# Ordering three weight conversions behind the first batch's layer norm

## The chip, the cores and the metric

The kernel runs on one core of a Trainium2 chip. The metric is the time of one execution on the device, in microseconds. The kernel before takes 1025.44 us, the median of three runs (1022.24 to 1027.12). The work is shared out to TensorE (PE, matrix multiplication, results to PSUM), VectorE (DVE), ScalarE (ACT), GpSimd (POOL) and SyncE (SP, whose queue issues all the DMAs here). Each engine runs its own list of instructions strictly in order; engines wait for each other on semaphores.

## The reference

Three blocks follow each other, over a batch of four, 768 tokens and 384 channels:

```
a_n  = a * min(|a|, 0.999) / (|a| + 1e-6)             # complex, per token, head and channel
S_t  = a_n[t] * S_(t-1) + outer(k_t, v_t)             # 48 x 48 per head, t = 0 .. 767
y_t  = q_t @ real(S_t)                                # block 1: gated linear attention
u    = y + real(fft(fft(y, tokens), channels))        # block 2: Fourier mixer
un   = (u - mean(u)) / sqrt(var(u) + 1e-6)            #          layer norm over 384 channels
x    = u + relu(un @ w_ch1) @ w_ch2                   #          MLP, 384 -> 1536 -> 384
u2   = x + (relu(x^T @ w_tok1) @ w_tok2)^T            # block 3: token mixing, 768 -> 256 -> 768
out  = u2 + relu(u2 @ w_ch1') @ w_ch2'                #          MLP, 384 -> 1536 -> 384
```

## The kernel before, in words

For each batch there is a *chain* (block 1 and the mixer up to the layer norm: a scan of 48 steps on DVE with preparations on ACT and POOL, then chunks of small matmuls on PE, then the DFT by folding, and the norm) and the *dense* work (transposes of the normalised tokens, the first MLP, token mixing, the second MLP). In the dense work every fp32 product is split into high and low fp32r parts, three matmuls of 128 x 128 by 128 x 384 each. It is 936 such matmuls per batch: 432 in each MLP and 72 in the token mixing. An MLP goes in four quarters; a quarter takes three weight pairs, has 54 matmuls of the first layer (L1034, 18 per weight) and then 54 of the second (L1056). The chain of batch b+1 is meant to run beside the dense work of batch b. The chain of batch 0 has nothing beside it.

The weights come from DRAM as 64-bit floats and are split on the chip by `convert` (L199 to L244): a load (L206, SP), two or three ACT passes into PSUM and SBUF (L214, L219, L222), a step on DVE (L225 or L227), an addition on POOL (L229), a second DVE step for some (L233), a rounding on ACT (L239), a subtraction on POOL (L240) and a store of the two halves into the scratch `wscr` (L244). It is a Python generator with a `yield` between the stages, and `tick` moves every open one a stage on. The two steps that read PSUM tile `p` take turns in two PSUM buffers, so that the third conversion's ACT step L214 waits for the first one's L233. Tiles `cvt` take turns in eight SBUF buffers of tag T, which the transposed tokens `th` and `tl` use as well.

Eight conversions of weights (`early`) are over before the mixer of batch 0. Two of the next twelve (`back`) follow. Eight more are open when the mixer begins: their loads and the ACT steps L219 are issued by then, and five calls of `tick` at the end of `mirrors` (after L1137) issue the rest. Two (8,1 and 10,1) are issued after the layer norm by `feed(56)`. The 36 other weights are converted while batch 0's dense work runs, each just ahead of its use; the first of them, w1 of pair 4, is used after 126 of the dense matmuls. Weights of `back` are read again from the scratch (L320).

Names of the layer norm: L1152 is the last DFT matmul, L1188 copies its result from PSUM on ACT, L1189 and L1190 (POOL) form difference and sum, L1204 (DVE) adds the transposed input, in three rounds of two token tiles; L1211 and L1212 are statistics, L1221 to L1226 the inverse square root, L1233 (DVE) or L1231 (ACT) the normalised tile `un`. Then L1012 transposes it on PE, L1017 (ACT) and L1018 (DVE) split it into `th` and `tl`, and the first MLP begins at L1034. L347 are filler matmuls on PE ("warm").

What sets the order: the framework's list scheduler goes over a simulated timeline and takes, among what is ready, the instruction of lowest rank (`RANK`: conversions and dense work stand behind the chain). `after(x, y)` adds a dependency for this ordering alone, without a semaphore. `rest(x)` is `after(x, rests[0])` for DVE steps of a conversion; `rests[1]` does the same for the POOL addition. What the scheduler decides in one place shifts everything that it places later.

Of the kernel before, what the change touches and what calls it, by code (L numbers as in the profile page):

```python
# [54 lines left out]
def attn_fft_mixer_kernel(ctx: ExitStack, tc: tile.TileContext, aL, xL, vL, wL, qN, kN, vN, arN, aiN,  # L55
# [109 lines left out]
    LAST = [None]  # L165

    def marked(x):
        if stream[0] != CHAIN:
            mark[0] = x

    def after(x, y):
        tc.add_manual_dep(x.ins, y.ins.name, HOLD, reason="order of the streams")
# [6 lines left out]
    rests = [None, None]  # L179
# [72 lines left out]
    active, begun = [], []  # L252

    def begin():
        p, j = convs.pop(0)
        return convert(p, j, ws.place if (p, j) in early else None, far=True)

    def feed(n):

        keep, stream[0] = stream[0], BACK  # L260
        for _ in range(n):
            if convs:
                for _ in begin():
                    pass
        stream[0] = keep

    def tick(n, loads=False):

        keep, stream[0] = stream[0], BACK
        active[:] = [g for g in active if next(g, "end") != "end"]  # L270
        for _ in range(n):
            g = begin()
            next(g)
            if not loads:
                next(g)
            active.append(g)
        stream[0] = keep
# [790 lines left out]
    def stage2(b, space):  # L1068
# [50 lines left out]
        def dft(kt):  # L1119
            for ty in range(4):  # L1120
                n0, n = 128 * kt, ZK[ty][kt]
                ps = palloc("s", [128, 2, 97])
                for r in range(2):
                    for dt in range(2):
                        te.matmul(out=ps[0:n, r, :], lhsT=fd[:, ty, r, dt, n0:n0 + n], rhs=dcos[0:112, ty % 2, dt, r, :],
                                  start=(dt == 0), stop=(dt == 1))
                se.copy(out=Z[0:n, 2 * ty + kt, :].rearrange("p (i r) -> p r i", r=2), in_=ps[0:n])
# [7 lines left out]
        if b == 0:  # L1135
            for o, v in kept:
                after(sp.dma_start(out=o, in_=v), x)  # L1137
            marked(x)
            rests[0], rests[1] = x, None
            for _ in range(5):  # L1140
                tick(0)
            rests[0] = None
        dft(0)

# [165 lines left out]
    def on(s, f, *args):  # L1310
        stream[0] = s
        return f(*args)

    def chain(b):
        return stage2(b, stage1(b))
# [2 lines left out]
    sp.dma_start(out=fk, in_=cFk)  # L1318
    u, norm = on(FIRST, chain, 0)
    t1 = on(FIRST, transposed, u, norm, "s")  # L1320
    feed(56)
    for b in range(B - 2):
        lent[0] = int(not b)
# [21 lines left out]
    with tc.If(fv != 0):  # L1345
        with tc.For_i(0, B, 1) as b:
            fallback(b)
            u, norm = stage2(B, alloc("qk", [128, 12288], name="ws"))
            t = transposed(u, norm, "s")
            dense2(B, u, *dense1(B, u, *t), row=b)  # L1350
# [111 lines left out]
```

## Time and profile before

| what | us |
|---|---|
| median of three runs | 1025.44 |
| the profiled execution's own time | 1025.11 |
| its span, first to last instruction | 1023.2 |
| first matmul of the first MLP starts | 155.15 |
| busy: PE, DVE, ACT, POOL | 951.0, 716.9, 526.4, 452.8 |
| mean granted clock of TensorE | 0.991 of full speed |

Times in the trace are counted from the first instruction. Matmuls overlap, so the sum of their lengths (some 340 ns each) is about twice the time in which they pass; their count in a window gives the pace. The granted clock is 1.00 at 2.4 GHz and 0.50 at 1.2 GHz.

### The profile page before, as it was taken

To read this page: it belongs to the slowest core of one execution; us is meant where nothing else is said; L and a number is where in the kernel's file an instruction comes from. 1 tells how busy PE (TensorE), PEld (TensorE's weight loads), DVE (VectorE), ACT (ScalarE), POOL (GpSimd) and SP (SyncE) were. 2 spreads that over 40 slices of the span, in tenths; PEclk is the share of its full clock that TensorE was granted. 3 is DMA by queue.
4 is the path that set the end of the run, shared out by engine and by line. 5 is a ranking of instruction groups with operands and counts; after the bars stand their busy time and mean duration, and the time that the engine had idled before them with its cause. 6 is when DMAs were issued, how large, how long until landed. Compare 5 with 4: busy or idle time off the path is not lost.

```text
span 1023.2 us, 21015 instructions
## 1 busy us (share of the span) xinstructions
PE 951.0 (93%) x7312; PEld 902.0 (88%) x7312; DVE 716.9 (70%) x1965; ACT 526.4 (51%) x1489; POOL 452.8 (44%) x655
## 2 busy tenths in 40 slices
PE   1479989999899999999999999999999999999997
PEld 0338869999898899999998999999989999999997
DVE  7988978889897778999668889855664333433332
ACT  7864568887995166887216667821342122211111
POOL 7744677765785673677147335614630002000000
PEclk9999999999999999999999999999999999999999
DMA  6625865886689435665734467553325345435422
GB/s 234 175 67 140 290 269 165 283 268 210 212 258 272 146 95 187 193 179 174 206 110 140 129 193 247 157 149 102 108 78 166 131 131 171 139 108 176 136 91 80
DMA packets 98337, 173.09 MB, mean 169 GB/s; under 512 B 10928, under 2 KB 57904, under 8 KB 97712
## 3 DMA queue, kind: packets, MB, share of 16 engines
q1 hardware_dynamic: 98224, 171.67, 53.8%
q8 instruction: 60, 0.98, 0.4%
q14 instruction: 53, 0.43, 0.1%
HBM read 132.31 MB, written 39.32 MB: 168 GB/s over the span
## 4 chain that ended last, share of the span: by engine, by line
PE 66%; DVE 6%; ACT 3%; DMA 2%; POOL 2%; issue 2%; SPq 0%; POOLq 0%; ACTq 0%; DVEq 0%
PE l L1056 25%; PE l L1034 23%; DMA cvt<-wL 2%; PE s L845 2%; PE s L721 2%; PE l L1260 1%; PE l L1278 1%; PE s L1260 1%; PE s L1278 1%; PE s L1152 1%; DVE qkt L1099 1%; PE s L900 1%; PE s L860 1%; PE c L721 1%; PE c L845 1%
## 5 line engine op out<-in xcount | busy, mean ns | idle before, releaser
L1056 PE MATMUL l<-w,h 128*128 128x384 f32 x1728 | 324.0, 339 | 1.5 <-DVE h L1047 1.0
L1034 PE MATMUL l<-th,w 128*128 128x384 f32 x1152 | 313.3, 341 | 2.8 <-DVE h L1047 2.5
L1056 PEld LDWEIGHTS l<-w,h 128*128 128x128 f32 x1728 | 298.2, 188 | 3.5 <-DVE h L1047 2.0
L1034 PEld LDWEIGHTS l<-th,w 128*128 128x128 f32 x1152 | 209.1, 188 | 5.8 <-DVE h L1047 3.9
L1038 ACT ACTIVATE h<-l 128x384 fp32r<-128x384 f32 x192 | 94.0, 490 | 215.9 <-PE l L1034 215.3
L1034 PE MATMUL l<-tl,w 128*128 128x384 f32 x576 | 194.6, 338 | 0.0
L1059 DVE TENSOR_TENSOR u<-u,l 128x384 f32<-128x384 f32 x192 | 105.5, 549 | 74.4 <-PE l L1056 73.4
L1047 DVE SCALAR_TENSOR_TENSOR h<-l,h 128x384 fp32r<-128x384 f32 x160 | 88.3, 552 | 88.9 <-ACT h L1038 88.8
L1034 PEld LDWEIGHTS l<-tl,w 128*128 128x128 f32 x576 | 108.4, 188 | 0.1
L229 POOL TENSOR_TENSOR cvt<-cvt 128x384 int32<-128x384 int32 x48 | 50.4, 1051 | 27.4 <-DVE cvt L225 16.5
L1245 POOL TENSOR_TENSOR xl<-u,xh 128x384 fp32r<-128x384 f32 x18 | 18.0, 1014 | 93.2 <-ACT xh L1244 93.0
L240 POOL TENSOR_TENSOR w<-cvt,w 128x384 fp32r<-128x384 f32 x44 | 45.0, 1027 | 13.1 <-ACT w L239 13.0
L1045 POOL TENSOR_TENSOR h<-full,h 128x384 fp32r<-128x384 f32 x32 | 32.5, 1016 | 34.3 <-ACT full L1044 32.8
L529 PE MATMUL s<-misc,y 128*112 128x128 f32 x64 | 14.5, 369 | 35.4 <-DVE y L511 27.9
L694 DVE TENSOR_TENSOR p<-p,A 128x144 f32<-128x144 f32 x144 | 44.7, 310 | 2.8 <-ACT A L671 1.0
L529 PEld LDWEIGHTS s<-misc,y 128*112 128x112 f32 x64 | 9.3, 177 | 41.6 <-POOL ss L496 20.3
L881 POOL TENSOR_TENSOR yc<-Aa,gm 48x384 f32<-48x384 f32 x18 | 20.6, 1147 | 53.3 <-DVE Aa L871 53.0
L670 POOL TENSOR_TENSOR A<-raw,tm 128x144 f32<-128x144 f32 (+1 forms) x51 | 25.9, 508 | 39.4 <-DVE yt L695 29.6
L696 DVE TENSOR_TENSOR p<-p,yt 128x96 f32<-128x96 f32 x144 | 37.7, 262 | 2.8
L651 POOL TENSOR_TENSOR tm<-tm 128x144 f32<-128x144 f32 (+1 forms) x51 | 25.3, 496 | 32.3 <-ACT tm L650 27.8
L695 DVE TENSOR_TENSOR yt<-p,A 128x96 f32<-128x96 f32 x144 | 36.2, 251 | 2.4 <-ACT A L674 0.5
L721 PE MATMUL s<-misc,y 128*112 128x128 f32 x222 | 35.5, 273 | 1.2 <-DVE y L708 0.8
(320 smaller groups left out, 2045.2 us busy)
## 6 DMA issues: line engine op xcount, KB each, us to landing
w<-wscr SPq DMA_DIRECT2D x180, 384.0 KB, 3.5
cvt<-wL SPq DMA_DIRECT2D x48, 384.0 KB, 4.8
wscr<-w SPq DMA_DIRECT2D x44, 384.0 KB, 4.1
Kn<-kn SPq DMA_DIRECT2D x56, 192.0 KB, 3.7
kn<-y SPq DMA_DIRECT2D x96, 96.0 KB, 2.7
raw<-aL SPq DMA_DIRECT2D x48, 144.0 KB, 3.8
xx<-xL SPq DMA_DIRECT2D x48, 144.0 KB, 3.6
V<-vL SPq DMA_DIRECT2D x32, 144.0 KB, 3.0
```

The source lines that it names most:

```text
L229: x = ge.tensor_tensor(out=a, in0=a, in1=lo, op=ALU.add)
L240: ge.tensor_tensor(out=parts[:, 1, :], in0=a.bitcast(F32), in1=r32(parts[:, 0, :]), op=ALU.subtract)
L694: ve.tensor_tensor(out=cur, in0=prev, in1=A[:, j, 0:3, :], op=ALU.mult)
L695: ve.tensor_tensor(out=y, in0=prev[:, 1::-1, :], in1=A[:, j, 3:5, :], op=ALU.mult)
L696: ve.tensor_tensor(out=cur[:, 0:2, :], in0=cur[:, 0:2, :], in1=y, op=ALU.add)
L721: te.transpose(ps[:, j, :], y[:, j, 0:112], ident)
L1034: te.matmul(out=ps, lhsT=w1[:, wi, kt * 128:kt * 128 + 128], rhs=x[g][:, kt, :], start=(n == 0), stop=(n == 8))
L1038: x = se.activation(out=hi, in_=ps, func=ACTF.Relu)
L1045: ge.tensor_tensor(out=lo, in0=full, in1=r32(hi), op=ALU.subtract)
L1047: ve.scalar_tensor_tensor(out=lo, in0=ps, scalar=0.0, in1=r32(hi), op0=ALU.max, op1=ALU.subtract)
L1056: te.matmul(out=ps, lhsT=hs[m][:, hi, tt * 128:tt * 128 + 128], rhs=w2[:, wi, :], start=(n == 0), stop=(n == 8))
L1059: ve.tensor_tensor(out=u[tt], in0=u[tt], in1=ps, op=ALU.add)
```

## The change

Of the eight open conversions the first five run on as before. The last three, cvt_1380, cvt_1382 and cvt_1384 in the built program (weights 15,1, 4,1 and 6,1), are set aside during the five ticks and put back into `active`. They are ticked after the transposes of batch 0 have been issued, with their DVE steps and the POOL addition ordered behind `LAST[0]`, the last normalised tile of batch 0 (L1231, token tile 5). What follows from these steps by data (L239, L240, the store L244) is behind it as well. Their loads and first ACT steps are issued where they were.

```
--- before.py
+++ after.py
@@ -1137,8 +1137,10 @@
                 after(sp.dma_start(out=o, in_=v), x)
             marked(x)
             rests[0], rests[1] = x, None
+            active[:], begun[:] = active[:5], active[5:]
             for _ in range(5):
                 tick(0)
+            active[:], begun[:] = begun[:], []
             rests[0] = None
         dft(0)
 
@@ -1318,6 +1320,10 @@
     sp.dma_start(out=fk, in_=cFk)
     u, norm = on(FIRST, chain, 0)
     t1 = on(FIRST, transposed, u, norm, "s")
+    rests[:] = [LAST[0]] * 2
+    for _ in range(5):
+        tick(0)
+    rests[:] = [None] * 2
     feed(56)
     for b in range(B - 2):
         lent[0] = int(not b)
```

(From here on, lines of the changed kernel are two higher than before between L1139 and L1322, and six higher behind.)

How the built programs differ. On DVE, in the layer norm of batch 0, the rows around the normalisation of the first token tile (u0) stood so before; cvt is a conversion's tile, p its PSUM tile:

```order
L227 TENSOR_SCALAR cvt_1384<-p_1473 128x384
L1204 TENSOR_TENSOR u1_1509<-s_1734,qkt_278 128x192
L1204 TENSOR_TENSOR u4_1512<-c_1743,qkt_278 128x192 x2
L1211 BN_STATS bst_1683<-u1_1509 128x6
L1225 TENSOR_TENSOR l_1712<-l_1712,rs_1685 128x2
L233 SCALAR_TENSOR_TENSOR cvt_1382<-p_1470,cvt_1382 128x384
L1211 BN_STATS bst_1683<-u4_1512 128x6
L1212 BN_AGGR mv_1684<-bst_1683 128x2
L1226 SCALAR_TENSOR_TENSOR rs_1685<-l_1712,rs_1685 128x2
L1212 BN_AGGR mv_1684<-bst_1683 128x2
L1233 TENSOR_SCALAR qkt_278<-u0_1508,mv_1684,rs_1685 128x384
```

Now the three conversions stand on DVE behind the last normalised tile there, between the splits of the transposed tokens (tl, th):

```order
L1018 TENSOR_TENSOR tl_1792<-s_1799,th_1790 128x3x128
L227 TENSOR_SCALAR cvt_1380<-p_1467 128x384
L227 TENSOR_SCALAR cvt_1382<-p_1470 128x384
L1018 TENSOR_TENSOR tl_1791<-c_1807,th_1789 128x3x128
L233 SCALAR_TENSOR_TENSOR cvt_1380<-p_1467,cvt_1380 128x384
L1018 TENSOR_TENSOR tl_1792<-s_1813,th_1790 128x3x128
L1018 TENSOR_TENSOR tl_1791<-s_1819,th_1789 128x3x128
L227 TENSOR_SCALAR cvt_1384<-p_1473 128x384
L1018 TENSOR_TENSOR tl_1792<-c_1825,th_1790 128x3x128
L233 SCALAR_TENSOR_TENSOR cvt_1382<-p_1470,cvt_1382 128x384
```

All six DVE instructions have moved; no conversion is left between the first statistics and the last normalised tile.

On SP's queue, the stores of the conversions (wscr) and the loads of the next (cvt from wL) stood so before, up to the first loads for weights that the dense work waits for (cvt_3574 is w1 of pair 4):

```order
L244 DMA wscr150_134<-cvt_1378 128x768
L244 DMA wscr151_135<-cvt_1380 128x768
L244 DMA wscr41_113<-cvt_1382 128x768
L244 DMA wscr61_117<-cvt_1384 128x768
L206 DMA cvt_1851<-wL 128x768
L206 DMA cvt_1862<-wL 128x768
L626 DMA raw_1920<-aL 128x288
L630 DMA xx_1922<-xL 128x288
L244 DMA wscr81_121<-cvt_1851 128x768
L244 DMA wscr101_125<-cvt_1862 128x768
L206 DMA cvt_3574<-wL 128x768
```

and now:

```order
L244 DMA wscr150_134<-cvt_1378 128x768
L206 DMA cvt_1851<-wL 128x768
L626 DMA raw_1920<-aL 128x288
L630 DMA xx_1922<-xL 128x288
L244 DMA wscr151_135<-cvt_1380 128x768
L206 DMA cvt_1862<-wL 128x768
L244 DMA wscr41_113<-cvt_1382 128x768
L244 DMA wscr61_117<-cvt_1384 128x768
L206 DMA cvt_3574<-wL 128x768
L244 DMA wscr81_121<-cvt_1851 128x768
L206 DMA cvt_3582<-wL 128x768
```

The loads of cvt_1862 and cvt_3574 now stand behind the stores of moved conversions.

## Rows read from the trace of the kernel before

**Rows 1.** the page, part 1: busy time, share and instructions.

```profile
PE 951.0 (93%) x7312; PEld 902.0 (88%) x7312; DVE 716.9 (70%) x1965; ACT 526.4 (51%) x1489; POOL 452.8 (44%) x655
```

**Rows 2.** windows of 20 us: length, busy us (count) by engine, clock, DMA.

```profile
160.00:180.00 20.00, 20.00 (x119) 19.92 (x118) 17.71 (x49) 17.76 (x52) 15.86 (x24) 1.00 0.63 212
...
380.00:400.00 20.00, 20.00 (x125) 19.15 (x124) 15.80 (x54) 10.56 (x29) 1.50 (x4) 1.00 0.36 110
```

**Rows 3.** waits of PE, 155 to 390 us: total us, times, longest.

```profile
PE l L1034 <- DVE h L1047: 2.3, 2, 1.6
PE p L1125 <- DVE qkt L1109: 1.7, 2, 1.5
PE s L845 <- DVE gt L813: 1.6, 1, 1.6
```

**Rows 4.** timeline of PE, start of the first MLP: start, length, line, operation.

```profile
155.15 1.34 PE L1034 MATMUL l<-th,w 128*128 128x384 f32 x3
...
157.89 0.51 PE L1034 MATMUL l<-th,w 128*128 128x384 f32 x2
```

**Rows 5.** windows of 2 us around it.

```profile
150.00:152.00 2.00, 2.00 (x4) 0.42 (x2) 1.15 (x5) 1.97 (x9) 0.00 (x0) 0.50 0.95 313
...
156.00:158.00 2.00, 2.00 (x13) 1.98 (x12) 1.08 (x3) 2.00 (x7) 1.17 (x2) 1.00 0.16 45
```

**Rows 6.** instruction groups, 126 to 155 us: busy, mean ns, idle before.

```profile
L229 POOL TENSOR_TENSOR cvt<-cvt 128x384 int32<-128x384 int32 x8 | 8.1, 1019 | 7.3 <-DVE cvt L227 7.3
L240 POOL TENSOR_TENSOR cvt<-cvt 128x384 fp32r<-128x384 f32 x8 | 8.0, 1005 | 2.3 <-ACT cvt L239 2.3
...
L233 DVE SCALAR_TENSOR_TENSOR cvt<-p,cvt 128x384 int32<-128x384 int32 x8 | 4.4, 551 | 2.3 <-POOL cvt L229 2.1
L227 DVE TENSOR_SCALAR cvt<-p 128x384 int32<-128x384 int32 x8 | 4.3, 552 | 1.5 <-ACT p L214 1.5
L239 ACT CAST cvt<-cvt 128x384 fp32r<-128x384 f32 x8 | 4.0, 501 | 1.1 <-DVE cvt L233 1.1
```

**Rows 7.** timeline of ACT.

```profile
140.89 0.48 ACT L1188 COPY qkt<-s 128x386 f32<-128x386 f32 x1
...
151.76 0.72 ACT L1231 ACTIVATE qkt<-u,rs 128x384 f32<-128x384 f32 x1
...
390.80 0.71 ACT L1231 ACTIVATE qkt<-u,rs 128x384 f32<-128x384 f32 x1
```

**Rows 8.** timeline of POOL.

```profile
142.56 1.01 POOL L229 TENSOR_TENSOR cvt<-cvt 128x384 int32<-128x384 int32 x1
143.53 0.53 POOL L1189 TENSOR_TENSOR qkt<-qkt 128x193 f32<-128x193 f32 x1
...
172.84 1.08 POOL L240 TENSOR_TENSOR w<-cvt,w 128x384 fp32r<-128x384 f32 x1
```

**Rows 9.** timeline of DVE.

```profile
143.45 2.26 DVE L1233 TENSOR_SCALAR qkt<-u,mv,rs 128x384 f32<-128x384 f32 x1
...
146.17 0.61 DVE L1204 TENSOR_TENSOR u<-s,qkt 128x192 f32<-128x192 f32 x2
...
151.17 0.48 DVE L1233 TENSOR_SCALAR qkt<-u,mv,rs 128x384 f32<-128x384 f32 x1
...
167.79 0.32 DVE L694 TENSOR_TENSOR p<-p,A 128x144 f32<-128x144 f32 x1
```

**Rows 10.** the window from the first scan step of POOL to L240.

```profile
152.88:173.92 21.04, 21.04 (x115) 20.11 (x114) 16.46 (x40) 18.93 (x53) 14.88 (x22) 0.93 0.44 146
```

**Rows 11.** timeline of PE, end of batch 0.

```profile
394.98 2.70 PE L1056 MATMUL l<-w,h 128*128 128x384 f32 x14
```

**Rows 12.** timeline of the DMA queue of SP.

```profile
148.55 0.88 SPq L206 DMA_DIRECT2D cvt<-wL  x2
...
163.87 2.62 SPq L206 DMA_DIRECT2D cvt<-wL  x4
```

**Rows 13.** DMA issues, 100 to 230 us: count, size, us to landing.

```profile
wscr<-cvt SPq DMA_DIRECT2D x12, 384.0 KB, 3.7
```

More of the change, by code (lines that the diff above doesn't have):

```diff
@@ L1139, in stage2 @@
             rests[0], rests[1] = x, None
+            active[:], begun[:] = active[:5], active[5:]
             for _ in range(5):
                 tick(0)
+            active[:], begun[:] = begun[:], []
             rests[0] = None
@@ L1320, in attn_fft_mixer_kernel @@
     t1 = on(FIRST, transposed, u, norm, "s")
+    rests[:] = [LAST[0]] * 2
+    for _ in range(5):
+        tick(0)
+    rests[:] = [None] * 2
     feed(56)
```

## The prediction, made before the changed kernel ran

> **What bounds the kernel now.** Read the page's busy times first: PE is busy for 951.0 of 1023.2 us [rows 1]. Then the windows of 20 us: from 160 to 180 PE passes 119 matmuls, nearly all dense, so one in 0.168 us, and from 380 us on it stands full (125 matmuls, some of them small) to the end [rows 2]. The end is thus the start of the first MLP, plus PE's fixed work, plus what PE waits behind that start. The waits between 155 and 390 us are 12 rows with 12.3 us in sum, of which the three largest stand in [rows 3]; behind 390 there is little. Third, the start: the first dense matmul begins at 155.15 and the 13th at 157.89 [rows 4]. Twelve at 0.168 us are 2.0, so PE is where a full-rate start at 155.9 would put it. The rest is clock: 0.50 granted from 150 to 152 us (1.2 GHz), 1.00 from 156 to 158 (2.4 GHz) [rows 5]; PE had waited for tiles of the layer norm before.
>
> So there are two questions: how much earlier PE starts, and whether it must wait more afterwards.
>
> **What leaves the layer norm.** Three conversions take with them 3 L227 and 3 L233 on DVE (6 x 0.55 = 3.3 us), 3 L229 and 3 L240 on POOL (3 x 1.019 + 3 x 1.005 = 6.1 us), 3 L239 on ACT (1.5 us) and three stores on SP [rows 6]. One L214 goes later too, as its PSUM buffer is freed later. None of this work disappears.
>
> What of it lay on the path? Follow the third round of the norm. Its copy L1188 comes from PE and stays: 140.89 + 0.48 = 141.37 [rows 7]. POOL's L1189 starts only at 143.53, because L229 of a moved conversion holds POOL from 142.56 [rows 8]. Without it the two additions of 0.53 end at 142.45, against 144.5: 2.1 us. On DVE, L1233 of the first tile takes 2.26 us beside these POOL instructions and 0.48 later, when POOL is idle; then a moved L233 follows, and L1204 of the third round starts at 146.17 [rows 9]. Now L1233 would be held at most until 142.45, end at 142.95, and with one small step L1204 starts at 143.1: 3.1 us earlier. From 146.17 to the last normalised tile (151.76 + 0.72 = 152.48) it is 6.3 us [rows 7, 9]; less an L239 in ACT's way, that tile is done at 149.0, 3.5 us earlier.
>
> On ACT two scan steps of about 0.4 and three L1017 of 0.48 follow: the first MLP can start at 151.1. But the order puts four ACT steps of conversions and scan, at the 0.50 of L239 some 2.0 us, ahead of the last L1017, which the tenth matmul needs: it comes at 153.5, nine matmuls are through at 152.6, PE waits 0.9. The effective start is 152.0 against 155.9: **-3.9**. Bounds: -2.1, if only POOL's share is won and the clock falls as before; -4.8 without the wait of 0.9.
>
> What this L1233 shows bears on the moved work too. The Trainium skill, SBUF — State Buffer, section SBUF: two separate sides, says that VectorE and GpSimd take a shared pair of ports as an exclusive lock, in some forms of operation, and the later one is blocked for the whole instruction. The trace agrees in the 2.26 us. By that rule the moved additions take the lock from the scan's DVE steps instead; it is the mechanism of the second rival.
>
> **What comes back behind it.**
> (a) *PE's wait for L813.* PE waits 1.6 us at L845, where the chain of batch 1 leaves its scan [rows 3]. Counted over the built programs, 747 dense matmuls stand ahead of that place before and 771 now: 24 x 0.168 = 4.0 us more cover, about as much as PE starts earlier. If the scan is no later than before, the wait goes: **-1.6** (bounds -1.6 and 0).
> (b) *The first weights converted in the MLP.* POOL's L240 for w1 of pair 4 ends at 172.84 + 1.08 = 173.9 [rows 8]; PE needs it after 126 matmuls, at 155.9 + 21.2 = 177.1. There were 3.2 us to spare. Now PE needs it at 173.2. From the first scan step to this L240 POOL was busy for 14.9 of 21.0 us [rows 10], and the moved 6.1 us join it. Starting at 149.3 (3.6 earlier, with the norm), they end at 170.3 if they fill all of POOL's idle time and at 176.4 if none. PE waits 0 to 3.2 us there; I take the middle, and as the next weights follow at the same distance nothing is won back: **+1.5**.
> (c) *The scan and the end of batch 0.* DVE is busy for 17.7 of 20 us at 160 to 180 [rows 2], and the scan's first step (167.79 before [rows 9]) has moved steps ahead of it, 3.3 us on DVE. I put it 2.5 us earlier, less than PE. Besides, 14 dense matmuls stood behind the last transposes of batch 1 [rows 11], and now none does, 2.4 us less cover; but the tile that they transpose was ready at 390.80 + 0.71 = 391.5 [rows 7], 3.2 us before PE turned to it. Other waits grow by 0 to 2.4: **+1.0**.
>
> The sum is -3.9 - 1.6 + 1.5 + 1.0 = -3.0. The profiled execution took 1025.1 us (its span and 1.9 around it), 0.3 below the median of the runs. I forecast 1022.
>
> **The rivals.**
> *PE alone decides.* All of POOL's idle time is used, (b) and (c) are 0, and L1034's waits for DVE (2.3 us, [rows 3]) shrink by half: -3.9 - 1.6 - 1.1 = -6.6, so 1018.5. For it: PE is full from 380 on. Against it: the loads below.
> *Given back in the scan.* The moved work of DVE and POOL slows the stretch in which DVE is 88% busy: 3.3 us of its own and up to 1.8 (2.26 - 0.48, [rows 9]) for a block, one such. That is 5.1, against the 5.5 of -3.9 and (a): the time stays at 1025. For it: conversions, scan and dense steps share DVE, ACT and POOL, and every one of them runs in order. Against it: the order has 24 more dense matmuls before the scan's end, so PE has work while it lasts.
> *Slower: SP's queue.* The loads cvt_1851 and cvt_1862 were issued together at 148.55, four loads of the next weights from 163.87 [rows 12]. Now cvt_1862 takes the buffer of cvt_1380 and waits until its store has landed (3.7 us [rows 13]); behind it stand two more moved stores and the load for w1 of pair 4. If POOL's 6.1 and this 3.7 both go into the stream of conversions, that weight comes at 173.9 + 9.8 = 183.7, 6.6 us after the old need of 177.1, and PE's early start is worth nothing: 1025.1 + 6.6 = 1032. It decides from the point at which L240 for w1 of pair 4 ends later than 177.1. Against it: POOL and the queue start 3.6 us earlier, and the store's landing lies beside POOL's other work.
> That the change doesn't do what it says is excluded by the order of DVE and SP: the steps have moved.
>
> **How the numbers follow.** Forecast 0.45, PE alone 0.22, given back 0.20, slower 0.13. About 0.5% (5.1 us) is what a measurement of this kernel tells from no change. Faster by more than that needs less than 1020.3: 0.8 of the PE case and a quarter of the forecast's, 0.29. Slower by more than that needs over 1030.6: most of the last case, 0.12. The rest, 0.59, is within. With the terms' bounds the forecast alone goes from 1018.7 (-4.8 - 1.6) to 1026.6 (-2.1 + 3.2 + 0.4); with most of the PE case and a part above, the range is 1017 to 1028.5.
>
> **What would show it.** In the profile after: the last normalised tile ends near 149 and the first L1034 starts near 151 (within 1 us), without a stretch of clock 0.50 as long as before; POOL's first addition of the third round follows its copy on ACT at once; w1 of pair 4 is done between 171 and 176; PE has little or no wait at L845 of batch 1, and the last matmul of batch 0 ends 2 to 4 us before 397.7. I am wrong if L1034 starts after 153.5, if PE's waits between there and 390 are over 15 us in sum, or if the difference arises behind 400 us, where I see nothing that changes.

## The result

The changed kernel takes 1033.96 us, the median of 11 runs (1029.37 to 1040.03), against 1025.11 for the kernel before on the same chip (11 runs, 1022.24 to 1027.12): a ratio of 1.0094, interval 1.0075 to 1.0112. It is slower by some 9 us, where 3 us less were forecast, and above the top of the range. The profiled execution took 1031.89 us (span 1030.0, granted clock 0.988), so its span is 6.8 us longer than before; the other 2 us between the medians are not in this trace.

The page of the changed kernel, part 1, has the same 7312 matmuls:

```profile
PE 955.5 (93%) x7312; PEld 904.5 (88%) x7312; DVE 716.1 (70%) x1965; ACT 526.7 (51%) x1489; POOL 453.9 (44%) x655
```

Against [rows 1] TensorE is busy 4.5 us longer with the same work and idle 2.3 us longer (1030.0 - 955.5 = 74.5 against 1023.2 - 951.0 = 72.2).

**The head came out as forecast.** The timelines of PE, ACT and POOL of the changed kernel: start, length, line, tiles.

```profile
150.94 0.74 PE L1034 MATMUL l<-th,w 128*128 128x384 f32 x1
```

```profile
140.86 0.48 ACT L1190 COPY qkt<-s 128x386 f32<-128x386 f32 x1 [1.22 <-PE s L1154]
...
147.71 0.71 ACT L1233 ACTIVATE qkt<-u,rs 128x384 f32<-128x384 f32 x1
...
151.70 0.51 ACT L1017 CAST th<-c 128x384 fp32r<-128x384 f32 x1
```

```profile
141.42 0.53 POOL L1191 TENSOR_TENSOR qkt<-qkt 128x193 f32<-128x193 f32 x1 [1.74 <-ACT qkt L1190]
...
171.52 2.06 POOL L240 TENSOR_TENSOR w<-cvt,w 128x384 fp32r<-128x384 f32 x2
```

POOL's addition follows its copy at once (141.42 behind 141.34), the last normalised tile is done at 148.4 (152.5 before, [rows 7]), and the first dense matmul starts at 150.94 instead of 155.15 [rows 4]. The traces of the experiments below agree: with the head of before (before, e2, e3, e8) the first dense matmul starts at 153.8 to 156.5 us, with the changed head (the changed kernel, e1, e5, e7, e9, e12, e13) at 150.5 to 153.9. Windows of 2 us of the changed kernel, in the columns of [rows 5], show the clock at its upper level where it had been at 0.50:

```profile
150.00:152.00 2.00, 1.91 (x9) 1.29 (x10) 1.99 (x5) 2.00 (x6) 2.00 (x4) 1.00 0.28 77
```

The waits of PE from 155 to 390 us, in the columns of [rows 3]:

```profile
PE l L1034 <- DVE h L1047: 3.5, 4, 1.9
PE l L1056 <- DVE h L1047: 1.8, 2, 1.2
PE l L1012 <- DVE u L1282: 1.4, 1, 1.4
PE s L860 <- DMA Kn<-kn: 1.3, 1, 1.3
```

L845's wait for L813 is gone. The ten rows add to 10.8 us; the twelve of before add to 10.3, not to the 12.3 of the prediction. The first h (L1038) is 4.6 us earlier than before, the 49th, at 397 us, still 2.1 us.

**The loss lies behind 480 us.** First the waits of PE from 480 to 800 us before, the rows of the layer norm, then those of the changed kernel:

```profile
PE c L1012 <- ACT qkt L1231: 0.8, 1, 0.8
PE s L1012 <- ACT qkt L1231: 0.5, 1, 0.5
```

```profile
PE s L1012 <- ACT qkt L1233: 3.8, 1, 3.8
PE s L860 <- DMA Kn<-kn: 2.5, 1, 2.5
```

Two waits are new in size: 2.5 us at 498 us, where the chunks of batch 2 need their first Kn, and 3.8 us at 767 us, where TensorE has no dense matmul left and waits for the layer norm of batch 3. Behind each the clock falls. Windows of the changed kernel (length, busy us and count of PE, PEld, DVE, ACT, POOL, clock, DMA), and two of them before:

```profile
496.00:500.00 4.00, 1.65 (x34) 1.63 (x35) 1.33 (x3) 0.00 (x0) 0.00 (x0) 0.95 0.66 202
500.00:504.00 4.00, 4.00 (x21) 3.89 (x21) 3.37 (x8) 0.48 (x1) 0.00 (x0) 0.62 0.77 203
...
764.00:768.00 4.00, 0.70 (x4) 0.71 (x5) 3.41 (x5) 3.24 (x8) 3.72 (x4) 0.73 0.46 174
768.00:772.00 4.00, 4.00 (x14) 4.00 (x14) 0.71 (x2) 1.07 (x2) 2.06 (x3) 0.50 0.02 4
```

```profile
500.00:504.00 4.00, 4.00 (x59) 3.74 (x59) 2.42 (x5) 0.95 (x2) 1.63 (x2) 1.00 0.65 183
...
768.00:772.00 4.00, 4.00 (x25) 4.00 (x24) 1.11 (x2) 0.55 (x2) 0.00 (x0) 1.00 0.38 105
```

Last, the chain's own clock: ACT's last normalised tile of batches 1, 2 and 3 in the changed kernel (the first column is its start), and of batches 2 and 3 before; that of batch 1 before is the last of [rows 7], 390.80.

```profile
392.45 0.71 ACT L1233 ACTIVATE qkt<-u,rs 128x384 f32<-128x384 f32 x1 [0.23 <-DVE rs L1232]
...
589.07 0.70 ACT L1233 ACTIVATE qkt<-u,rs 128x384 f32<-128x384 f32 x1
...
768.19 0.71 ACT L1233 ACTIVATE qkt<-u,rs 128x384 f32<-128x384 f32 x1 [0.95 <-DVE rs L1232]
```

```profile
583.42 0.71 ACT L1231 ACTIVATE qkt<-u,rs 128x384 f32<-128x384 f32 x1 [0.23 <-DVE rs L1230]
...
762.22 0.70 ACT L1231 ACTIVATE qkt<-u,rs 128x384 f32<-128x384 f32 x1
```

From the last of these to the end of the span it is 261.0 us before and 261.8 after. So the 6.8 us are: 1.65 late at batch 1, 4.0 more from batch 1 to batch 2, 0.3 from there to batch 3, 0.8 behind. The 1.65 is within what executions differ by: e9 and e12 below have the changed kernel's order up to there, and in their traces that tile starts at 398.7 and 393.1. TensorE's dense work is 3.2 us early at 479 us (its 1369th matmul) and 2.1 us late at 590 (its 1657th).

Where batch 2 loses its 4.0 us is seen at its stations: the first and the last step of its scan (the 48 steps on DVE), the first matmul of the chunks (L803) and the first that needs Kn (L860). Before, then the changed kernel:

```profile
397.27 0.32 DVE L694 TENSOR_TENSOR p<-p,A 128x144 f32<-128x144 f32 x1
484.59 0.31 DVE L694 TENSOR_TENSOR p<-p,A 128x144 f32<-128x144 f32 x1
...
488.71 0.65 PE L803 MATMUL s<-misc,ends 128*48 128x64 f32 x16
494.95 0.26 PE L860 MATMUL s<-V,Kn 96*64 96x48 f32 x1
```

```profile
396.38 0.32 DVE L694 TENSOR_TENSOR p<-p,A 128x144 f32<-128x144 f32 x1
486.56 0.31 DVE L694 TENSOR_TENSOR p<-p,A 128x144 f32<-128x144 f32 x1
...
488.96 0.43 PE L803 MATMUL s<-misc,ends 128*48 128x64 f32 x8
498.35 0.23 PE L860 MATMUL s<-V,Kn 96*64 96x48 f32 x1 [2.53 <-DMA Kn<-kn]
```

The scan starts 0.9 us earlier than before and ends 2.0 us later; the chunks begin 0.25 us late, their first Kn product 3.4 us, and the norm comes 5.65 us late.

The two built programs also differ in what stands ahead of the chain in TensorE's queue. Number of dense matmuls there (the last columns: how many stand between the chain's last transposes L1199 of batch 3 and TensorE's stop for the last normalised tiles, behind the 2304th):

| dense matmuls ahead of | before | after | cover of the last norm, before | after |
|---|---|---|---|---|
| first L803 (chunks begin), batches 1, 2, 3 | 747, 1399, 2068 | 771, 1412, 2079 | | |
| first L1125 (mixer), batches 1, 2, 3 | 824, 1507, 2199 | 854, 1530, 2213 | | |
| last L1199, batch 3 | 2260 | 2272 | 44 | 32 |

24 to 30 more dense matmuls stand ahead of the chain of batch 1 and 13 to 23 more ahead of that of batch 2. That the chain is late because it stands behind them is not what the traces show. From the last y of the scan (L708) to the first L803 it is 6.1 us in both kernels at batch 1 (302.22 to 308.31 before, 306.33 to 312.41 now), and at batch 2 it is 4.5 us before (484.22 to 488.71) and 2.8 now (486.19 to 488.96): it is the scan that ends later. The last columns do bear on the last norm: 12 matmuls less of cover are 2.0 us at 0.168 [rows 2], and the wait there is 2.5 us longer (3.8 against 0.8 + 0.5).

### The profile page after: what moved, and what is told of

Read it like the earlier page. It is cut to its first block, busy times and chain, and to the rows that moved or that the text cites. A ratio compares the mean times of both kernels' runs of the same rounds, so it can differ in the third digit from the quotient of the medians.

```text
span 1030.0 us, 20993 instructions
## 1 busy us (share of the span) xinstructions
PE 955.5 (93%) x7312; PEld 904.5 (88%) x7312; DVE 716.1 (70%) x1965; ACT 526.7 (51%) x1489; POOL 453.9 (44%) x655
## 4 chain that ended last, share of the span: by engine, by line
PE 45%; DVE 3%; POOL 1%; DMA 1%; ACT 1%; issue 1%; POOLq 0%; SPq 0%
PE l L1034 17%; PE l L1056 17%; PE s L845 1%; PE s L1262 1%; PE s L1280 1%; POOL qkt L1109 1%; DMA kn<-y 1%; PE s L721 1%; PE s L900 1%; DVE qkt L1099 1%; PE s L1154 1%; PE c L845 1%; PE s L1012 1%; PE s L860 0%; PE s L906 0%
## 5 line engine op out<-in xcount | busy, mean ns | idle before, releaser
L1038 ACT ACTIVATE h<-l 128x384 fp32r<-128x384 f32 x192 | 94.4, 493 | 210.2 <-PE l L1034 209.6
L240 POOL TENSOR_TENSOR w<-cvt,w 128x384 fp32r<-128x384 f32 x44 | 45.6, 1044 | 15.9 <-ACT w L239 15.6
```

Source lines behind the costliest of these rows:

```text
L240: ge.tensor_tensor(out=parts[:, 1, :], in0=a.bitcast(F32), in1=r32(parts[:, 0, :]), op=ALU.subtract)
L1038: x = se.activation(out=hi, in_=ps, func=ACTF.Relu)
```

## The experiments

Theory A: the loss comes from the order behind the change. Rival B: it comes from the moved steps, which load the scan of batch 1. Most runs use a table of an engine's instructions by their numbers of issue in another built program; each is ordered behind its predecessor there, by dependencies without a semaphore, so that a stretch can be given the order of either kernel:

```
-            return getattr(self.eng, name)
+            return wrapped(getattr(self.eng, name), pin)   # pin(x) after each instruction
...
+            if a in made and b in made:                    # a, b: neighbours in the table
+                tc.add_manual_dep(made[b].ins, made[a].ins.name, HOLD, reason="order of before")
```

All times, with the stages of the chain in the profiled execution (start of the last normalised tile, as above). Each ratio is to runs of before on the same chip; the row of before is that of the first comparison.

| run | median us | ratio to before, interval | profiled us | batch 1 | 1 to 2 | 2 to 3 | 3 to end |
|---|---|---|---|---|---|---|---|
| before | 1025.1 | | 1025.1 | 390.8 | 192.6 | 178.8 | 261.0 |
| changed | 1034.0 | 1.0075 to 1.0112 | 1031.9 | 392.4 | 196.6 | 179.1 | 261.8 |
| e1_order_before | 1032.9 | 1.0060 to 1.0105 | 1031.1 | 396.5 | 192.9 | 178.8 | 261.0 |
| e2_order_after | 1034.5 | 1.0080 to 1.0120 | 1040.7 | 399.4 | 199.2 | 179.1 | 261.2 |
| e3_null | 1039.0 | 1.0111 to 1.0152 | 1039.8 | 392.6 | 195.7 | 179.1 | 270.5 |
| e4_move_two | 1030.3 | 1.0038 to 1.0071 | 1030.8 | 389.7 | 196.5 | 182.5 | 260.3 |
| e5_conv_free | 1029.7 | 1.0027 to 1.0059 | 1028.5 | 394.3 | 192.6 | 178.8 | 260.9 |
| e6_two_free | 1027.8 | 1.0014 to 1.0049 | 1026.8 | 392.8 | 192.6 | 178.8 | 260.8 |
| e7_kn_early | 1047.8 | 1.0201 to 1.0248 | 1047.5 | 403.8 | 198.7 | 179.2 | 264.0 |
| e8_null_act | 1036.1 | 1.0070 to 1.0126 | 1036.0 | 392.1 | 196.9 | 178.3 | 266.8 |
| e9_before_from_batch2 | 1025.7 | 0.9978 to 1.0015 | 1029.0 | 398.7 | 189.1 | 178.8 | 260.7 |
| e10_head_plus4 | 1032.7 | 1.0045 to 1.0100 | 1032.6 | 394.2 | 196.2 | 179.1 | 261.2 |
| e11_one_free | 1028.6 | 1.0004 to 1.0045 | 1030.8 | 396.3 | 192.9 | 178.8 | 261.1 |
| e12_before_from_batch3 | 1031.4 | 1.0037 to 1.0081 | 1029.4 | 393.1 | 197.0 | 176.8 | 260.8 |
| e13_sp_batch2 | 1039.5 | 1.0116 to 1.0161 | 1036.2 | 393.7 | 199.1 | 179.1 | 262.5 |

The stages of batch 2 go by the order. In the runs that have the order of before from its scan on (before, e1, e5, e6, e9, e11) the scan lasts 86.1 to 87.3 us and from its end to the norm it is 98.8 to 99.1; in those with the order of the changed kernel (changed, e2, e7, e10, e12, e13) it is 90.2 to 90.5 and 101.8 to 104.9.

**e1_order_before.** The changed kernel, all five engines in the order of before from the first instruction of the `feed` on; only the three conversions stand where the change puts them.

> The changed kernel up to the first layer norm and with the three moved conversions, but every instruction issued from the feeding of the remaining conversions on stands on each engine in the order of the kernel before (order-only dependencies). Theory A (the loss comes from the order that the scheduler made behind the change): the first dense matmul near 151 us as in the changed kernel, no PE wait of 2 us or more at 498 or at 767 us, total 1021 to 1025 us. Theory B (the loss is the moved steps themselves, which make the scan of batch 1 late by 3.5 us at 204 us): total 1030 to 1034 us, with the scan of batch 1 late by 3 us or more.

1032.9: neither late wait is there (the norm of batch 3 waits 0.8 and 0.5 us, as before), and behind 200 us the trace is that of before, 5.7 to 7.5 us late. But theory A's time is missed, and B's numbers came out (1030 to 1034, the last step of batch 1's scan at 308.8 instead of 302.6): another loss, at 158 us, took the place. PE's wait, then ACT and SP of the same run:

```profile
PE l L1034 <- DVE h L1047: 6.7, 1, 6.7
```

```profile
163.72 0.51 ACT L214 ACTIVATE p<-cvt 128x384 f32<-128x384 f32 x1 [4.70 <-DMA cvt<-wL]
164.16 0.53 ACT L219 ACTIVATE cvt<-cvt 128x384 int32<-128x384 uint32 x1
164.59 0.40 ACT L648 ACTIVATE tm<-tm,lnc 128x144 f32<-128x144 f32 x1
164.90 0.40 ACT L649 ACTIVATE tm<-tm,lnc 128x144 f32<-128x144 f32 x1
165.20 0.47 ACT L1038 ACTIVATE h<-l 128x384 fp32r<-128x384 f32 x1
```

```profile
156.87 2.28 SPq L244 DMA_DIRECT2D wscr<-cvt  x2
159.25 0.37 SPq L206 DMA_DIRECT2D cvt<-wL  x1
```

The second weight load of the `feed`, issued right behind the first of 148.55 before [rows 12], goes out at 159.25, behind the store of the moved conversion whose tile it takes. ACT waits for it in line, and with it the scan's steps (tm) and the first h of the MLP. The Trainium skill, Perfetto Trace Analysis, section Tensor Engine Instruction (MATMUL, LD_WEIGHTS), says that ACT, DVE and GpSimd run strictly first in, first out; the 4.70 us in front of L214, with L1038 in line behind it, agree.

**e2_order_after.** The reverse: the kernel before, its conversions not moved, in the order of the changed kernel from the same place on.

> The kernel before, its three conversions not moved, but from the same point on in the order of the changed kernel. Theory A: slower than before by as much as the changed kernel or more, since the gain at the head is missing: 1031 to 1038 us, with PE waits near 500 and 770 us. Theory B: 1024 to 1027 us, as before.

1034.5 (the traced execution is the longest of the five), and both late waits are back without a moved conversion:

```profile
PE s L860 <- DMA Kn<-kn: 4.6, 1, 4.6
PE s L1012 <- ACT qkt L1231: 3.8, 1, 3.8
```

So the order makes these waits (theory A), and the moved steps are not needed for them.

**e3_null.** One added line in the kernel before:

```
     t1 = on(FIRST, transposed, u, norm, "s")
+    warm(1, ident, LAST[0])
```

> The kernel before with one more matmul of 128 columns behind the first layer norm, nothing moved on purpose. If an order that comes out otherwise by chance is worth several us either way (theory A in its widest form): off by 3 us or more from 1025, in either direction; its order has the chain of batch 1 behind 674 dense matmuls, not 747, so rather faster: 1015 to 1022. Theory B and any theory in which only the moved steps count: 1025 within 1.5 us.

1039.0: 14 us for one matmul of 128 columns (two records in the trace, 0.38 us together), in the direction that I had not expected. The chain of batch 1 stands behind 674 dense matmuls, and now TensorE waits for the chain in the middle (waits of PE, 300 to 480 us), while dense work is left over at the end: 270.5 us behind the norm of batch 3, where 1496 dense matmuls remain instead of 1440 (56 at 0.168 us are 9.4 of the 9.5 us).

```profile
PE p L845 <- DVE sc L852: 3.6, 2, 3.0
PE p L1125 <- ACT sq L638: 3.0, 1, 3.0
```

**e4_move_two.**

```
-            active[:], begun[:] = active[:5], active[5:]
+            active[:], begun[:] = active[:6], active[6:]
```

> The changed kernel with two conversions moved behind the layer norm instead of three. Theory B: two thirds of the loss, 1030 to 1031 us. Theory A: its order has the chain of batch 1 behind 693 dense matmuls, not 771, and of batch 3 behind 2042, not 2079, so the chain is early and the gain at the head stays: 1015 to 1023 us.

1030.3, B's number, but not for B's reason: its order is another one (693 dense matmuls ahead of the chain of batch 1), its first dense matmul starts at 155.9, so the head gains nothing, and PE waits 2.9 us for Kn. It does not tell the theories apart.

**e5_conv_free, e6_two_free, e11_one_free.** As e1, with the steps of `convert` left out of the table; three, two and one conversion moved.

```
-ORDER: all of before's instructions from the feed on
+ORDER: the same without those of lines 197 to 252
```

> As e1 (changed kernel, from the feeding on in the order of before), but the steps of the conversions are left out of the fixed order, so only the chain and the dense work stand as in before. In e1 TensorE waited 6.7 us for h at 158 us because ScalarE's L214 waited 4.7 us for a weight load whose tile a moved conversion still held. Theory C (the three conversions hold their tiles, so the next weight loads and what stands behind them in ScalarE's queue are late): the scheduler now puts L214 later, the 6.7 us wait is under 2 us, the scan of batch 1 is less than 3 us late, total 1022 to 1027 us. Theory D (the chain and the dense work in the order of before can't be had with three conversions moved, wherever their steps stand): 1031 to 1034 us.

> As e5 with two conversions moved instead of three, so that the tiles of the next two weight loads are not among the moved ones and both loads stand ahead of the moved stores in SyncE's queue. Theory C: no wait of ScalarE for a weight load of 2 us or more before 170 us, as in before; the total is that of before less what of the 4 us of the head is kept: 1021 to 1025 us. Theory D: 1028 us or more.

> As e6 with one conversion moved instead of two (chain and dense work in the order of before, conversions free). e5 with three lost 4.9 us against before, e6 with two 3.0 us. If each conversion moved into the scan of batch 1 costs 1.5 us or so there, more than the head gives back: 1025.5 to 1027 us. If one conversion fits in idle time of VectorE and GpSimd and the head still gains: 1021 to 1024 us, faster than both kernels.

1029.7, 1027.8 and 1028.6. The wait of 6.7 us is gone and a part of the loss (theory C); e5 and e6 end between the numbers of C and D. From batch 1 on all three repeat the stages of before (192.6 or 192.9, 178.8, 261); what they lose they lose ahead of the norm of batch 1 (394.3, 392.8, 396.3 against 390.8). A price per conversion does not come out: e11, with one, is slower than either of its numbers, and its first dense matmul starts at 155.9, no gain at the head (in a traced execution 2.2 us longer than its median). None is faster than before.

**e7_kn_early, e13_sp_batch2.** The changed kernel with four engines held in its own order; on SP alone kn's stores and Kn's loads stand up to three places earlier (e7), or the transfers issued from batch 2's scan up to batch 3's stand among each other as before (e13).

```
-SP: ... kn wscr cvt kn wscr cvt wscr kn ...
+SP: ... kn kn wscr cvt kn wscr cvt wscr ...        # e7
```

> The changed kernel with TensorE, VectorE, ScalarE and GpSimd fixed to their own order (nothing moves there); only on SyncE each store of kn and load of Kn behind batch 1's scan stands up to three places earlier, ahead of stores and loads of weights. If SyncE's order makes the late Kn (1.3 us of TensorE's wait at 321, 2.5 us at 498) and by it the late layer norm of batch 3: both waits under 0.7 us, the wait of 3.8 us at 767 us under 2 us, total 1027 to 1030 us. If the scan itself is late: the same waits and 1032 to 1036 us.

> The changed kernel with TensorE, VectorE, ScalarE and GpSimd fixed to their own order; on SyncE alone the transfers issued from the scan of batch 2 up to that of batch 3 stand among each other in the order of before. If the late Kn comes from SyncE's queue and makes the loss of batch 2: no wait for Kn above 0.7 us at 498 us, batch 2's normalization at most 3 us later than before, total 1025 to 1028 us. If the loss comes from the chain standing behind 13 to 23 more dense matmuls on TensorE and from the order of the other engines: batch 2's normalization still 4 us or more late, 1030 to 1035 us.

1047.8 and 1039.5, both worse. The wait for Kn at 498 us is gone in both, and a wait for a weight of the token mixing stands in its place (waits of PE from 480 to 800 us, first e7, then e13):

```profile
PE l L1262 <- DMA w<-wscr: 4.0, 1, 4.0
PE s L1012 <- ACT qkt L1233: 3.8, 1, 3.8
```

```profile
PE l L1262 <- DMA w<-wscr: 3.9, 1, 3.9
PE s L1012 <- ACT qkt L1233: 3.8, 1, 3.8
```

SP's queue serves both; what one transfer gains, another loses, and with the other engines unchanged the chain is no earlier. With SP's order of before in batch 2 (e13) the scan still lasts 90.4 us, so its length does not come from SP. e7 loses most ahead of batch 2: its batch 1 is 11.4 us later than in the changed kernel, with a new wait at 311 us (waits of PE, 155 to 480 us):

```profile
PE s L721 <- DVE y L708: 5.7, 1, 5.7
```

**e8_null_act.** Four copies of one column in the kernel before, behind the first norm; no buffer changes.

```
+    for _ in range(4):
+        after(se.copy(out=chk[:, 2:3], in_=eps), LAST[0])
     feed(56)
```

> The kernel before with four copies of one column (some 0.1 us each) on ScalarE behind the first layer norm, nothing moved on purpose and no buffer changed; its order comes out otherwise (the chain of batch 1 behind 684 dense matmuls, not 747). If the order that the scheduler finds is what the time hangs on: 1030 us or more, as e3 (1039). If e3 was slow for its one more TensorE buffer: 1025 to 1027 us.

1036.1: e3 was not slow for its PSUM buffer. Two harmless additions cost 11 and 14 us because the order came out otherwise. Here too dense work is left over: 1476 dense matmuls stand behind the last norm, 36 more than before, 6.0 us at 0.168, and the end is 5.8 us further behind it.

**e9_before_from_batch2, e12_before_from_batch3.** The changed kernel left as it is up to the scan of batch 2 (e9) or of batch 3 (e12), and from there in the order of before.

> The changed kernel as it is up to the scan of batch 2; every instruction issued from that scan on stands in the order of before. In the changed kernel the last normalization of batch 1 ends 1.6 us later than before, that of batch 2 5.7 us, that of batch 3 6.0 us, and from that one to the end of the span it is 261 us in both. If the order behind batch 1 makes the greater part of the loss: no wait of 2.5 us for Kn at 498 us and none of 3.8 us at 767 us, batches 2 and 3 end their normalization 0 to 2 us later than before, total 1024 to 1028 us. If the loss comes from batch 1 (moved steps in its scan) and is only seen later: batch 3 still 5 to 7 us late, 1031 to 1034 us.

> As e9, but only what is issued from the scan of batch 3 on stands in the order of before; batches 1 and 2 stay in the changed kernel's own order. If the loss that e9 took away arises in the order of batch 2 (chain behind 13 to 23 more dense matmuls, wait of 2.5 us for Kn at 498 us): that wait stays, the normalization of batch 2 ends 4 us or more later than before, total 1029 to 1033 us. If it arises in the order of batch 3 alone: 1024 to 1027 us, as e9.

e9 takes 1025.7 us: the loss is gone, with all three conversions moved. The profiled execution took 1029.0 (the twelve go from 1023.2 to 1030.7); it is late by 8.0 us at batch 1, in the order that was 1.65 late in the changed kernel's trace, and by 4.4 at batch 3. The waits of PE from 480 to 800 us, first e9, then e12:

```profile
PE c L1012 <- ACT qkt L1233: 0.8, 1, 0.8
PE s L1012 <- ACT qkt L1233: 0.5, 1, 0.5
```

```profile
PE s L860 <- DMA Kn<-kn: 2.7, 1, 2.7
...
PE c L1012 <- ACT qkt L1233: 0.8, 1, 0.8
```

e12 takes 1031.4: with batch 2 in the changed kernel's order the wait for Kn and the 197.0 us from batch 1 to batch 2 stay, and only the wait at the last norm goes. So the order of batch 2 makes 5.7 us of the loss (1031.4 - 1025.7), that of batch 3 the 2.6 up to the changed kernel's 1034.0. By the ratios to before on the same chip it is 6.4 and 3.6 us, each give or take 3, so the second is hardly clear of noise. The clock of e12 stays at its upper level behind the wait for Kn, which begins at 496.7 us, so the 197.0 do not need a fall of the clock:

```profile
496.00:500.00 4.00, 1.35 (x33) 1.22 (x33) 1.66 (x5) 0.48 (x1) 0.00 (x0) 1.00 0.67 188
500.00:504.00 4.00, 4.00 (x46) 3.81 (x43) 3.43 (x7) 0.48 (x1) 0.00 (x0) 1.00 0.66 164
```

**e10_head_plus4.** All engines fixed to the changed kernel's own order, and the gain at the head taken back:

```
+    for _ in range(3):
+        warm(5, ident, LAST[0])
     feed(56)
```

> The changed kernel with every engine fixed to its own order and 15 more matmuls of 128 columns (4.1 us) on TensorE between the first layer norm and the first dense matmul, which takes the gain at the head back. If TensorE's lead of the head is given back anyway, because the chain sets when batch 3's normalization ends: within 1.5 us of the changed kernel (1032 to 1035 us), the wait at 767 us gets shorter. If the lead at the head carries through TensorE's in-order queue to the end: 3 to 4 us more, 1036 to 1038 us.

The added matmuls on TensorE:

```profile
152.09 3.51 PE L347 MATMUL l<-misc 128*128 128x128 f32 x30
```

1032.7 against 1034.0 for the changed kernel: 3.5 us more work on TensorE, with the first dense matmul at 155.36 instead of 150.94, cost nothing that stands out from noise, and the 3 to 4 us of the other case are outside the interval. In this order the lead is worth nothing, since the end is 261 us behind the norm of batch 3. Against my expectation the wait at 767 us did not get shorter; it is 3.8 us again, and that norm comes 1.3 us later. The run also shows that holding an order costs nothing by itself.

## Why the prediction was wrong

- *Layer norm head, -3.9.* Right: the first h comes 4.6 us earlier. POOL's share was as described; L1235 of the first tile took 0.62 us, which made the norm's end 0.6 earlier than forecast. The wait of 0.9 did not come: the last L1017 ends at 152.2, ahead of the tenth matmul.
- *(a) -1.6.* The wait for L813 is gone, as said. But the condition, a scan that is no later than before, did not hold: its last step stands at 306.69 instead of 302.59, and at the chunks of batch 1 PE waits 1.3 us for Kn in the place of the 1.6.
- *(b) +1.5.* No wait: L240 for w1 of pair 4 ends at 172.5, and the 127th dense matmul, which needs it, starts at 174.72. Within the bounds of 0 to 3.2.
- *(c) +1.0.* The ten waits add to 10.8 us against 10.3 before, so the whole of (a), (b) and (c) is +0.5 by the waits, where +0.9 was put. At 397 us the lead is 2.1 us, not 3.0. That this is near is partly luck: in e12 and e9, which have the same order up to there, the 49th h comes at 398.0 and 403.7 us, against 397.2 in the changed kernel and 399.3 before.
- *The step that failed* is the first: "The end is thus the start of the first MLP, plus PE's fixed work, plus what PE waits behind that start", with "behind 390 there is little". It took the order behind 390 us as given and a busy TensorE as the bound. Of the 4.7 us of waits behind 390 in the trace before, 1.3 stand at the last layer norm: TensorE was there before the chain already. A longer lead of the dense work only lengthens that wait and is worth nothing (e10; e9, which keeps the changed head and the moved conversions, is not faster than before either), and every microsecond by which the chain is late counts in full: 260.3 to 262.5 us lie behind the last norm in all runs but the nulls and e7. The term left out is the chain's delay behind 390 us, +4.0 from batch 1 to 2, and 0.3 + 0.8 behind; with the order of before from batch 2 on it is gone (e9, 1025.7).
- What the 4.0 consist of is shown in part. The changed kernel's order makes the scan of batch 2 some 3 us longer and the way from its end to the norm 3 to 6 us longer in every run that has it; 2.5 us are won back by a scan that starts sooner behind the norm of batch 1 (3.9 us instead of 6.5). The wait of 2.5 us for Kn lies on that way, but e7 and e13 show that it can't be taken out by itself. The half clock behind it is not needed (e12). Which engine's order lengthens the scan stays open: it is not SyncE's alone (e13), and no run gives one of the other engines alone the order of before.
- *The rivals.* "Slower: SP's queue" has the right sign and the wrong place. Its mechanism cost nothing in the changed kernel, where w1 of pair 4 is in time. In e1 a load does wait for a moved conversion's store, but it acts by way of ACT's queue on the first h and not by a late weight, so that its 6.7 us stand beside the 6.6 of the rival's price by chance. "Given back": the scan of batch 1 does take 6.2 us longer (165.73 to 306.69, before 167.79 to 302.59), but this is not the loss, since e9 has the same order there and loses nothing; the head's gain is given back at the last norm. That the order comes out worse by itself was not among the rivals, and e3 and e8 show that it was likely: all four edits that left the order free (the change, e3, e4, e8) made this kernel 6 to 14 us slower.
- I had named "if the difference arises behind 400 us, where I see nothing that changes" as what would prove me wrong. It could have been seen: of VectorE's 1965 places at least 1134 hold another instruction in the two built programs, 660 of them behind 400 us.

## What to carry to other kernels

Where a list scheduler sets the order and two streams meet at a join, look at the wait at that join before the change. Here TensorE already waited 1.3 us there for the chain: by this a lead of the dense work, won 600 us earlier, is worth nothing, and an earlier chain some 1.3 us at most (an estimate from that wait; no run has a chain that is earlier there). Compare the built order over the whole program, and count on both sides of the join: too little cover ahead of it is a wait (32 dense matmuls instead of 44, 3.8 us instead of 1.3), and dense work left behind it is time at the end (36 and 56 more, 5.8 and 9.5 us, in e8 and e3). An edit of such a kernel is to be measured against null edits, or with the rest of the order held fixed, before its own effect is believed.

## What the runs showed that was not expected

- A wait of 2.5 us on TensorE was followed by a window of 4 us at a mean clock of 0.62, one of 3.8 us by 4 us at 0.50 (1.2 GHz); the two waits of 0.8 and 0.5 us before left it at 1.00. The same place shows that a wait of this size is not always followed by a fall: the 2.7 us in e12 left the clock at 1.00, while 1.9 us in e10 were followed by 4 us at a mean of 0.57. Behind the 3.8 us at the last norm it fell in all five traces that have this wait and the changed kernel's order (changed, e2, e7, e10, e13).
- L1235 of the first tile, which had taken 2.26 us [rows 9], took 0.62 us beside both of POOL's additions (141.54 to 142.16, POOL from 141.42 on). So these additions alone do not hold it for their whole length, as my reading of 2.26 us had it. In e4, where it began beside a conversion's L240 and both additions followed, it took 1.27 us. What decides is not shown.
